# Attention and two feed-forward layers on one core: PSUM as eight one-bank tiles behind the first product, another sharing of the first pair's banks, and later squares

## The chip, the cores and the metric

The kernel runs on one core of one Trainium2 chip. Its engines are TensorE (PE in the profile), VectorE (DVE), ScalarE (ACT), GpSimd (POOL) and SyncE (SP, which here only starts loads and stores). They run side by side and meet at semaphores. The metric is the time of one execution on the device in microseconds. The kernel before takes 766.9 us (median of 3 runs, 766.66 to 767.11).

## The reference

```python
def _attn_ref(q, k, v, centroids):          # q, k, v: 2 x 8 x 768 x 64
    ...                                     # q_n, k_n, c_n: normalised rows
    q_assign = np.argmax(np.einsum('bhsd,hcd->bhsc', q_n, c_n), axis=-1)
    k_assign = np.argmax(np.einsum('bhsd,hcd->bhsc', k_n, c_n), axis=-1)
    mask = q_assign[:, :, :, None] == k_assign[:, :, None, :]
    scores = np.where(mask, scale * np.matmul(q, k.transpose(0, 1, 3, 2)), -1e9)
    ...                                     # softmax over the last axis
    return np.matmul(attn, v)

def _moe_ref(x, w_in, w_out):               # x: 1536 x 512, w_in: 512 x 2048
    h = np.maximum(x @ w_in, 0.0)
    return h * h @ w_out

def _moe2_ref(x, w_in, w_out):
    h = x @ w_in
    g = h * (1.0 / (1.0 + np.exp(-1.702 * h)))
    return g @ w_out
```

The attention's output, 1536 tokens of 512 numbers, goes through the first layer (relu, squared) and then through the second (a gelu). Each layer has a first product with `w_in` and a second one with `w_out`.

## The kernel before

**The order.** The kernel is written under a manual schedule. Each piece of work is recorded by `at(key, f, ...)`, all pieces are sorted by their key, and in that order they are issued to the engines. `moment(u)` turns a count of steps into a key; one step `u` of the two layers is 2.7 us of PE work. Each engine works its own instructions off in the order of their issue. What an instruction has to wait for is worked out while it is recorded, from the tiles that it reads and writes.

**The first layer's first product** (`first_hidden`, L831, with `first_product`, L787). `w_in` has 16 blocks of 128 columns, taken as eight pairs `j`. Each pair is computed by seven products of half-size blocks instead of eight, in the order P1, P2, P6, P5, P7, P3, P4. Every number is a sum of a high and a low part, so one product of 384 columns is six matmuls (`PASSES`). The results of the seven products run together in three accumulators: u (P1, P6, P7, P4 one after the other), c (P2) and x (P5, P3). Between them ACT copies an accumulator out (`first_take`, L811), or DVE adds it to a copy (`first_plus`, L816), and only then PE goes on adding into it. ACT also does the relus (L819, L823, and L827 with Relu) and the squares (L827 with Square). In pair 0 the two batches b are done one after the other, with 384 columns each; from pair 1 on both come together, twelve matmuls a product, and one copy or add takes both (768 elements).

**PSUM.** A partition of PSUM has eight banks of 512 numbers. The attention uses tiles of two banks (`ps_s`) and of one. For batch 0 of pair 0 the first product borrows two `ps_s` tiles (named `ps_h`), with u and c in the two banks of one and x in the other. Then `open_banks` (L760) closes the attention's pool and opens four tiles of two banks, `row0` to `row3`; `banks[i]` is half of `row{i // 2}`. For batch 1 of pair 0, u and c are the two halves of `row0` and x is a half of `row1`; from pair 1 on u, c and x are a whole row tile each. Everything behind, that is both second products (`reduce_out`, L976 to L981) and the second layer's first product (`product`, L869, for two of three column blocks, and `plain`, L878, for the third), uses single halves as accumulators, with ACT and DVE reading out (L886, L889, L883; L990, L1010, L1014, L1025).

**The weights** come as 64-bit numbers and are turned into a high and a low part on the way (`pair_stages`, L250 to L305): ACT L270, DVE L273 to L284, then ACT L288 and a difference L291 on POOL or DVE (the raw halves), four sums L296, ACT L299 and a difference L302. Pairs 0 and 1 have L291, L296 and L302 on POOL, the others on DVE. `PAIR_N` (L67) holds the keys of these steps; `rest_2` are those of L288, L291, L296, L299 and L302 of pair 2.

The second products split their moving operand in the same way: ACT L964 writes the high part, DVE L968 the low part, and PE reads both.

Of the kernel before, what the change touches and what calls it, by code (L numbers as in the profile page):

```python
# [8 lines left out]
F32 = mybir.dt.float32  # L9
# [3 lines left out]
AF = mybir.ActivationFunctionType  # L13
# [54 lines left out]
    load=-4.0, steps_1=(-1.0, -0.3, -0.2, -0.1, 0.0), steps_2=(-0.55, -0.3, 0.0, 0.3, 0.6), steps=(-1.95, -1.25, -0.9, -0.35, 0.0),  # L68
    rest_1=(3.2, 3.5, 3.7, 4.28, 4.5), rest_2=(1.0, 1.3, 1.95, 3.1, 4.1), rest=(0.85, 1.2, 1.95, 2.6, 3.0),
)  # L70
# [12 lines left out]
def cluster_attention_then_two_ffns(  # L83
# [224 lines left out]
    with tc.manual_schedule():  # L308
        with ExitStack() as actx:
            psum = actx.enter_context(tc.tile_pool(name="psum", bufs=1, space=bass.MemoryType.PSUM))  # L310
# [449 lines left out]
            def open_banks():  # L760
                actx.close()
                pool = ctx.enter_context(tc.tile_pool(name="psum2", bufs=1, space=bass.MemoryType.PSUM, reuse_waits="tile"))
                rows.extend(pool.tile([P, 2, CH], F32, name=f"row{i}") for i in range(4))
                banks.extend(rows[i // 2][:, i % 2, :] for i in range(8))

# [8 lines left out]
            def first_sum(name, j, b):  # L774
                i = "ucx".index(name)
                if j:
                    return first_banks(j)[i][:, b, :HALF]
                if b:
                    return banks[i][:, :HALF]
                if (i // 2, "early") not in ps_u:  # L780
                    ps_u[i // 2, "early"] = ps_s("ps_h")
                return ps_u[i // 2, "early"][:, i % 2, :HALF]

# [47 lines left out]
            def first_hidden(u0):  # L831
                cursor = u0
                for j in range(MJ):
                    for group in (((0,), (1,)) if j == 0 else ((0, 1),)):
                        b = group[0] if len(group) == 1 else None
                        for name in FIRST_ORDER:
                            for x in group:
                                at(moment(cursor), first_product, name, j, x)
                                cursor += BLOCK
                            end = cursor  # L840
                            if name in ("P1", "P6", "P5"):
                                at(moment(end + 0.02), first_take, name, j, b)
                            elif name in ("P2", "P7", "P3"):
                                at(moment(end + 0.02), first_plus, name, j, b)
                                if name == "P7":
                                    at(moment(end + 0.36), first_relu, 1, j, 1, b)
                                if name == "P3":
                                    at(moment(end + 0.36), first_whole, 0, j, b, AF.Relu)
                                    at(moment(end + 0.9), first_whole, 0, j, b, AF.Square)
                            else:  # L850
                                at(moment(end + 0.02), first_relu_banked, name, j, b)
                                at(moment(end + 1.2), first_whole, 1, j, b, AF.Square)

# [189 lines left out]
            at(moment(7 * BLOCK) - 0.01, open_banks)  # L1043
            first_hidden(u0)
            for j in range(MJ):
                places_ = ((32 * KB, 40 * KB), (26 * KB, 34 * KB))[j] if j < 2 else (98 * KB, 106 * KB) if j % 2 else (0, 8 * KB)
# [127 lines left out]
```

## Time and profile before

| | |
|---|---|
| median of 3 runs | 766.9 us |
| profiled execution | 766.83 us |
| its span, first to last instruction | 765.0 us |
| mean granted clock of TensorE | 0.999 |
| PE busy | 750.6 us (98%) |
| DVE, ACT, POOL busy | 525.5, 461.8, 165.6 us |
| L981, both second products | 262.4 us of PE |
| L793, first layer's first product | 110.9 us of PE in `row` tiles, 8.5 in `ps_h` |
| L869 and L878, second layer's first product | 81.8 and 48.2 us of PE |

PE is busy nearly all the time, so the table says which stretches are long, and not what a change in one of them is worth. A matmul here lasts longer than the distance to the next (389 ns of 128x512 against some 227), because matmuls overlap in the array. A stretch is therefore judged by its length over its number of matmuls, and a stall by how much longer it is than a free stretch. The attention ends and the first product begins near 250 us, the first layer's second product begins at 376.5, the second layer's first product at 507.8, its second one at 628.9.

### The profile page before, as it was taken

How to read it: one execution, taken by the hardware profiler on the slowest of the kernel's cores; microseconds unless marked ns; L12 is line 12 of the kernel's file. 1: busy time of each engine (PE TensorE's matmuls, PEld its weight loads, DVE VectorE, ACT ScalarE, POOL GpSimd, SP SyncE). 2: the span in 40 equal slices, each digit the busy share in tenths (PEclk: the TensorE clock that was granted, in tenths of full speed). 3: DMA queues.
4: the chain of work that ended last, by engine and by line, in shares of the span. 5: the costliest groups of instructions: out<-in, count | busy, mean ns of one | idle time of the engine just before them, and what ended most of it. 6: DMA issues, size and time to landing. Idle time of an engine off the chain costs nothing.

```text
span 765.0 us, 10778 instructions
## 1 busy us (share of the span) xinstructions
PE 750.6 (98%) x3995; PEld 605.3 (79%) x3995; DVE 525.5 (69%) x939; ACT 461.8 (60%) x800; POOL 165.6 (22%) x139
## 2 busy tenths in 40 slices
PE   8899999999999999999999999999999999999997
PEld 5677776766767789999988887888888878888786
DVE  6876866867886567665777768744777667776321
ACT  7877777786777567776854435545656554443321
POOL 3764756774758130000000000000000000000000
PEclk9999999999999999999999999999999999999999
DMA  5132321322320221301222320100212213230201
GB/s 187 43 104 56 96 79 42 101 72 56 96 87 3 73 93 56 111 4 53 82 99 96 111 83 15 41 23 34 82 56 84 82 56 98 95 111 28 110 1 55
DMA packets 17044, 54.53 MB, mean 71 GB/s; under 512 B 2592, under 2 KB 2848, under 8 KB 15968
## 3 DMA queue, kind: packets, MB, share of 16 engines
q1 hardware_dynamic: 16704, 53.32, 21.6%
q8 instruction: 31, 0.51, 0.3%
q10 hardware_dynamic: 288, 0.52, 0.2%
q14 instruction: 21, 0.17, 0.1%
HBM read 43.02 MB, written 3.15 MB: 60 GB/s over the span
## 4 chain that ended last, share of the span: by engine, by line
PE 86%; DVE 7%; ACT 4%; issue 1%; POOL 1%; DMA 0%; DVEq 0%; ACTq 0%; POOLq 0%
PE row L981 32%; PE row L793 11%; PE row L869 10%; PE ps_v L649 8%; PE ps_p L631 7%; PE row L878 5%; PE ps_s L606 5%; PE ps_s L609 4%; DVE arena L615 1%; PE ps_aff L467 1%; ACT arena L623 1%; PE ps_r L666 1%; PE ps_back L484 1%; ACT arena L827 1%; DVE arena L997 1%
## 5 line engine op out<-in xcount | busy, mean ns | idle before, releaser
L981 PE MATMUL row<-arena 128*128 128x512 f32 x1152 | 262.4, 389 | 0.7 <-DVE arena L1025 0.6
L981 PEld LDWEIGHTS row<-arena 128*128 128x128 f32 x1152 | 215.9, 188 | 46.8 <-DVE arena L1025 1.0
L615 DVE TENSOR_SCALAR_CACHE_REDUCE arena<-ps_s 128x768 bf16<-128x768 f32 x96 | 91.7, 955 | 39.1 <-PE ps_s L609 11.4
L793 PE MATMUL row<-arena 128*128 128x384 f32 x630 | 110.9, 335 | 2.1 <-ACT arena L811 2.1
L793 PEld LDWEIGHTS row<-arena 128*128 128x128 f32 x630 | 109.0, 188 | 3.8 <-ACT arena L811 3.7
L964 ACT CAST arena<-arena 128x512 fp32r<-128x512 f32 x96 | 59.4, 620 | 86.2 <-PE row L981 85.9
L623 ACT ACTIVATE arena<-ps_s,arena 128x768 f32<-128x768 f32 x96 | 87.2, 908 | 36.1 <-DVE arena L615 35.8
L968 DVE TENSOR_TENSOR arena<-arena,arena 128x512 fp32r<-128x512 f32 x96 | 66.1, 689 | 60.2 <-ACT arena L964 60.0
L869 PE MATMUL row<-arena 128*128 128x512 f32 x336 | 81.8, 391 | 0.2 <-DVE arena L889 0.2
L869 PEld LDWEIGHTS row<-arena 128*128 128x128 f32 x336 | 62.7, 188 | 14.8 <-DVE arena L889 1.3
L649 PE MATMUL ps_v<-arena 128*64 128x384 f32 x384 | 72.3, 498 | 0.0
L631 PE MATMUL ps_p<-arena 128*128 128x128 f32 x576 | 70.8, 272 | 0.0
L244 ACT CAST arena<-arena 128x512 fp32r<-128x512 f32 x48 | 29.8, 620 | 64.4 <-DVE arena L240 64.4
L631 PEld LDWEIGHTS ps_p<-arena 128*128 128x128 f32 x576 | 65.7, 141 | 2.3 <-issue 0.6
L606 PE MATMUL ps_s<-arena 128*128 128x384 f32 x192 | 54.8, 366 | 2.5 <-ACT arena L623 2.4
L609 PE MATMUL ps_s<-arena 80*128 80x384 f32 x192 | 49.9, 340 | 0.1
L247 DVE TENSOR_TENSOR arena<-arena,arena 128x512 fp32r<-128x512 f32 x48 | 33.2, 692 | 24.2 <-ACT arena L244 23.4
L878 PE MATMUL row<-arena 128*128 128x512 f32 x192 | 48.2, 390 | 0.0
L606 PEld LDWEIGHTS ps_s<-arena 128*128 128x128 f32 x192 | 31.1, 189 | 20.5 <-ACT arena L623 10.1
L639 DVE COPY arena<-ps_p 128x512 f32<-128x512 f32 x72 | 47.0, 678 | 0.2 <-PE ps_p L631 0.2
L649 PEld LDWEIGHTS ps_v<-arena 128*64 128x64 f32 x384 | 23.4, 136 | 25.5 <-issue 25.2
L827 ACT ACTIVATE arena<-arena 128x1536 f32<-128x1536 f32 (+1 forms) x27 | 36.3, 1346 | 10.1 <-DVE arena L816 10.1
(133 smaller groups left out, 953.0 us busy)
## 6 DMA issues: line engine op xcount, KB each, us to landing
arena<-in_w_dram SPq DMA_DIRECT2D x48, 512.0 KB, 3.2
arena<-in_w_dram SPq DMA_DIRECT2D x8, 1024.0 KB, 4.8
arena<-arena SPq DMA_DIRECT2D x32, 192.0 KB, 2.6
arena<-in_k_t_dram SPq DMA_DIRECT2D x8, 384.0 KB, 3.8
arena<-in_v_dram SPq DMA_DIRECT2D x8, 384.0 KB, 3.3
out_dram<-arena SPq DMA_DIRECT2D x11, 256.0 KB, 2.1
arena<-in_q_t_dram SPq DMA_DIRECT2D x7, 384.0 KB, 3.4
arena<-arena SPq DMA_DIRECT2D x28, 48.0 KB, 2.1
```

The costliest lines, as they stand in the source:

```text
L606: nc.tensor.matmul(ps[:, n, :HALF], lhsT=x_s[i][:, t * P:(t + 1) * P], rhs=k1_s[i][:, n * HALF:(n + 1) * HALF], start=True, stop=False)
L609: nc.tensor.matmul(ps[:, n, :HALF], lhsT=q2_s[i][:, t * P:(t + 1) * P], rhs=k2_s[i][:, n * HALF:(n + 1) * HALF], start=False, stop=True)
L615: nc.vector.tensor_scalar(out=unused, in0=s_t[g][:, :, :HALF], scalar1=-scale, scalar2=None, op0=ALU.mult, op1=ALU.min, accum_out=m_t[g])
L623: nc.scalar.activation(out=p_t[g].rearrange("p (n f) -> p n f", n=2), in_=s_t.pop(g)[:, :, :HALF], func=AF.Exp, bias=m_t.pop(g), scale=sca ...
L631: nc.tensor.transpose(ps[:, x * P:(x + 1) * P], p_t[2 * k + j][:, t * P:(t + 1) * P], ident)
L649: nc.tensor.matmul(pv_t[n][j * D:(j + 1) * D, :HALF], lhsT=raw[n // 2, "v"][:, j, t, :], rhs=pt_t[n, j][:, t, :], start=(t == 0), stop=(t ...
L793: nc.tensor.matmul(ps, lhsT=w[:, a, (off + x) * P:(off + x + 1) * P], rhs=FIRST_MOVING[moving, b][x][:, e, :], start=(n == 0 and name in ( ...
L869: nc.tensor.matmul(ps, lhsT=w[:, a, off + x * P:off + (x + 1) * P], rhs=MOVING[moving][x][:, b, :], start=(n == 0 and name in ("P1", "P2", ...
L878: nc.tensor.matmul(ps, lhsT=w[:, a, kk * P:(kk + 1) * P], rhs=THIRD_CHUNK[kk][:, b, :], start=(n == 0), stop=(n == 11), skip_group_check=True)
L964: nc.scalar.copy(out=half_of(layer, n)[:, 0, :], in_=g_t[m][:, c, :])
L968: nc.vector.tensor_tensor(out=t[:, 1, :], in0=g_t[m][:, c, :], in1=t[:, 0, :].bitcast(F32), op=ALU.subtract)
L981: nc.tensor.matmul(ps, lhsT=lhsT, rhs=rhs, start=(m == 0 and e == 0), stop=(m == MF - 1 and e == 2))
```

## The change

Three things change. First, the accumulators of pair 0 are shared out otherwise: u has a two-bank tile to itself, c and x are the two halves of another. Second, when the first layer's first product is over, the four row tiles are given back and eight tiles of one bank each take their place at the same addresses (`split_banks`). Third, in pairs 0, 1 and 2 the second layer of work on a copied block, relu and square, gets later keys (`later`: 3, 2 and 1 steps), and pair 2's weight split gets later keys too (`rest_2`). The relu that reads an accumulator itself (`first_relu_banked`) is recorded a little earlier, so that in the last pair it comes before the pool is closed. The added lines shift the names of lines by up to 7: L793, L811, L816, L819, L823 and L827 of before are L798, L816, L821, L824, L828 and L832 of the changed kernel, and L981 is L987.

```diff
-    rest_1=(3.2, 3.5, 3.7, 4.28, 4.5), rest_2=(1.0, 1.3, 1.95, 3.1, 4.1), rest=(0.85, 1.2, 1.95, 2.6, 3.0),
+    rest_1=(3.2, 3.5, 3.7, 4.28, 4.5), rest_2=(2.33, 2.4, 2.5, 3.2, 4.1), rest=(0.85, 1.2, 1.95, 2.6, 3.0),
...
             def open_banks():
                 actx.close()
-                pool = ctx.enter_context(tc.tile_pool(name="psum2", bufs=1, space=bass.MemoryType.PSUM, reuse_waits="tile"))
+                pool = rctx.enter_context(tc.tile_pool(name="psum2", bufs=1, space=bass.MemoryType.PSUM, reuse_waits="tile"))
                 rows.extend(pool.tile([P, 2, CH], F32, name=f"row{i}") for i in range(4))
-                banks.extend(rows[i // 2][:, i % 2, :] for i in range(8))
+
+            def split_banks():
+                rctx.close()
+                pool = ctx.enter_context(tc.tile_pool(name="psum3", bufs=1, space=bass.MemoryType.PSUM, reuse_waits="tile"))
+                banks.extend(pool.tile([P, CH], F32, name=f"bank{i}") for i in range(8))
...
                 if b:
-                    return banks[i][:, :HALF]
-                if (i // 2, "early") not in ps_u:
-                    ps_u[i // 2, "early"] = ps_s("ps_h")
-                return ps_u[i // 2, "early"][:, i % 2, :HALF]
+                    return rows[(i + 1) // 2][:, i // 2, :HALF]
+                t = (i + 1) // 2, "early"
+                if t not in ps_u:
+                    ps_u[t] = ps_s("ps_h")
+                return ps_u[t][:, i // 2, :HALF]
...
+                later = (3.0, 2.0, 1.0) + (0.0,) * MJ
...
-                                    at(moment(end + 0.36), first_relu, 1, j, 1, b)
+                                    at(moment(end + 0.36 + later[j]), first_relu, 1, j, 1, b)
...
-                                    at(moment(end + 0.36), first_whole, 0, j, b, AF.Relu)
-                                    at(moment(end + 0.9), first_whole, 0, j, b, AF.Square)
+                                    at(moment(end + 0.36 + later[j]), first_whole, 0, j, b, AF.Relu)
+                                    at(moment(end + 0.9 + later[j]), first_whole, 0, j, b, AF.Square)
...
-                                at(moment(end + 0.02), first_relu_banked, name, j, b)
-                                at(moment(end + 1.2), first_whole, 1, j, b, AF.Square)
+                                at(moment(end - 0.02 * (j == MJ - 1) + 0.01), first_relu_banked, name, j, b)
+                                at(moment(end + 1.2 + later[j]), first_whole, 1, j, b, AF.Square)
...
+            at(moment(y0 - 0.005), split_banks)
```

PE, POOL and SP issue their instructions in the same order as before; DVE swaps one pair of neighbours (pair 1's L816 on c now stands before pair 2's L291).

ACT at batch 0 of pair 0, before, with what each waits for (`ps_h` 2570 holds u and c, 2614 x; L811 are the copies of u behind P1 and P6 and of x behind P5):

```order
L811 COPY arena_112640_59<-ps_h_2570 128x384 [waits PE_49]
L670 COPY arena_112640_59<-ps_r_2579 128x384
L811 COPY arena_112640_59<-ps_h_2570 128x384 [waits DVE_49]
L695 CAST arena_114688_58<-arena_112640_59 128x384 [waits DVE_49]
L811 COPY arena_112640_59<-ps_h_2614 128x384 [waits PE_49]
```

And in the changed kernel (2570 holds u, 2592 c and x):

```order
L816 COPY arena_112640_59<-ps_h_2570 128x384 [waits PE_49]
L670 COPY arena_112640_59<-ps_r_2579 128x384 [waits PE_49]
L816 COPY arena_112640_59<-ps_h_2570 128x384 [waits PE_49]
L695 CAST arena_114688_58<-arena_112640_59 128x384 [waits DVE_49]
L816 COPY arena_112640_59<-ps_h_2592 128x384 [waits PE_49]
```

The order is the same; the second copy of u waits for PE and no longer for DVE's add.

ACT from pair 1's raw weights (L288) to pair 1's first copy of u (`row_2665`, 768 elements), before (`row_2663` and `row_2664` are rows 0 and 1, with batch 1 of pair 0):

```order
L288 CAST arena_58<-arena_59 128x768
L827 ACTIVATE arena_59<-arena_59 128x768
L811 COPY arena_59<-row_2663 128x384
L827 ACTIVATE arena_59<-arena_59 128x768
L811 COPY arena_59<-row_2664 128x384
L299 CAST arena_58<-arena_59 128x1024
L270 ACTIVATE arena_59<-arena_59 128x1024
L823 ACTIVATE arena_59<-arena_59 128x384
L827 ACTIVATE arena_59<-arena_59 128x768
L819 ACTIVATE arena_59<-row_2663 128x384
L827 ACTIVATE arena_59<-arena_59 128x768
L811 COPY arena_59<-row_2665 128x2x384
```

And in the changed kernel (rows 0, 1 and 2 are 2661, 2662 and 2663):

```order
L288 CAST arena_58<-arena_59 128x768
L816 COPY arena_59<-row_2661 128x384
L816 COPY arena_59<-row_2662 128x384
L299 CAST arena_58<-arena_59 128x1024
L270 ACTIVATE arena_59<-arena_59 128x1024
L828 ACTIVATE arena_59<-arena_59 128x384
L824 ACTIVATE arena_59<-row_2661 128x384
L832 ACTIVATE arena_59<-arena_59 128x768
L816 COPY arena_59<-row_2663 128x2x384
```

Before, four relus and squares of 768 elements (L827) stand between L288 and the copy, now one (L832), and it is batch 0's.

PE where the second layer's last column block begins (L981, from the last matmuls of the block before it), before; `row_2663` to `row_2666` are rows 0 to 3:

```order
L981 MATMUL row_2666<-arena_58 128x512 x3
L981 MATMUL row_2663<-arena_58 128x512 [waits Activation_49]
L981 MATMUL row_2663<-arena_58 128x512 x2
L981 MATMUL row_2666<-arena_58 128x512 [waits DVE_49]
L981 MATMUL row_2666<-arena_58 128x512 x2
L981 MATMUL row_2665<-arena_58 128x512 x6
L981 MATMUL row_2663<-arena_58 128x512 [waits Activation_49]
```

And in the changed kernel (`bank_3507` to `bank_3514` are banks 0 to 7):

```order
L987 MATMUL bank_3514<-arena_58 128x512 x3
L987 MATMUL bank_3508<-arena_58 128x512 x3
L987 MATMUL bank_3513<-arena_58 128x512 x3
L987 MATMUL bank_3511<-arena_58 128x512 [waits Activation_49]
L987 MATMUL bank_3511<-arena_58 128x512 [waits DVE_49]
L987 MATMUL bank_3511<-arena_58 128x512
L987 MATMUL bank_3512<-arena_58 128x512 [waits DVE_49]
```

The last six matmuls of the old block (banks 1 and 6) wait for nobody; the new block's first ones wait for the readers of their own banks.

## Rows read from the trace of the kernel before

**Rows 1.** The page: busy time; costliest groups (busy, mean ns | idle before, releaser)
```profile
PE 750.6 (98%) x3995; PEld 605.3 (79%) x3995; DVE 525.5 (69%) x939; ACT 461.8 (60%) x800; POOL 165.6 (22%) x139
...
L981 PE MATMUL row<-arena 128*128 128x512 f32 x1152 | 262.4, 389 | 0.7 <-DVE arena L1025 0.6
...
L793 PE MATMUL row<-arena 128*128 128x384 f32 x630 | 110.9, 335 | 2.1 <-ACT arena L811 2.1
```
**Rows 2.** The waits of PE: us in total, times, longest
```profile
PE row L793 <- ACT arena L811: 2.1, 5, 0.8
```
**Rows 3.** Timeline of PE, first products: start, length, instructions, count [idle before, releaser]
```profile
254.52 1.32 PE L793 MATMUL ps_h<-arena 128*128 128x384 f32 x6
...
257.85 2.38 PE L793 MATMUL ps_h<-arena 128*128 128x384 f32 x12
260.40 3.43 PE L793 MATMUL ps_h<-arena 128*128 128x384 f32 x18 [0.17 <-ACT arena L811]
263.68 2.24 PE L793 MATMUL row<-arena 128*128 128x384 f32 x12
266.49 2.36 PE L793 MATMUL row<-arena 128*128 128x384 f32 x12 [0.57 <-ACT arena L811]
269.04 7.65 PE L793 MATMUL row<-arena 128*128 128x384 f32 x42 [0.19 <-ACT arena L811]
277.47 4.46 PE L793 MATMUL row<-arena 128*128 128x384 f32 x24 [0.79 <-ACT arena L811]
282.09 10.68 PE L793 MATMUL row<-arena 128*128 128x384 f32 x60 [0.16 <-ACT arena L811]
...
293.17 83.50 PE L793 MATMUL row<-arena 128*128 128x384 f32 x480 [0.41 <-ACT arena L811]
```
**Rows 4.** Timeline of ACT, first products
```profile
255.87 0.48 ACT L811 COPY arena<-ps_h 128x384 f32<-128x384 f32 x1 [0.60 <-PE ps_h L793]
...
259.87 0.48 ACT L811 COPY arena<-ps_h 128x384 f32<-128x384 f32 x1 [3.14 <-DVE arena L816]
...
265.96 0.48 ACT L811 COPY arena<-row 128x384 f32<-128x384 f32 x1
266.33 0.84 ACT L288 CAST arena<-arena 128x768 fp32r<-128x768 f32 x1
...
274.80 0.83 ACT L827 ACTIVATE arena<-arena 128x768 f32<-128x768 f32 x1
...
276.64 0.79 ACT L811 COPY arena<-row 128x768 f32<-128x768 f32 x1
...
290.96 1.48 ACT L827 ACTIVATE arena<-arena 128x1536 f32<-128x1536 f32 x1
```
**Rows 5.** Timeline of DVE, first pair
```profile
259.28 0.56 DVE L816 TENSOR_TENSOR arena<-ps_h,arena 128x384 f32<-128x384 f32 x1 [4.25 <-issue]
```
**Rows 6.** Timeline of PE, the first layer's second product
```profile
376.51 131.42 PE L981 MATMUL row<-arena 128*128 128x512 f32 x576
```
**Rows 7.** Timeline of DVE where the first layer's last column block begins
```profile
464.41 0.69 DVE L990 COPY arena<-row 128x512 f32<-128x512 f32 x1 [0.67 <-ACT arena L990]
...
477.43 0.69 DVE L968 TENSOR_TENSOR arena<-arena,arena 128x512 fp32r<-128x512 f32 x1
```
**Rows 8.** The chain that ended last: start, length, what; second layer's first product
```profile
513.39 3.03 PE row L869 x12
...
519.14 2.72 PE row L869 x12
...
543.77 3.01 PE row L869 x12
...
619.02 1.54 PE row L878 x6
...
627.41 1.65 PE row L869 x6
```
**Rows 9.** Timeline of PE, the second layer's last column block
```profile
716.09 44.50 PE L981 MATMUL row<-arena 128*128 128x512 f32 x195 [0.63 <-DVE arena L1025]
```

More of the change, by code (lines that the diff above doesn't have):

```diff
@@ L308, in cluster_attention_then_two_ffns @@
     with tc.manual_schedule():
-        with ExitStack() as actx:
+        with ExitStack() as actx, ExitStack() as rctx:
             psum = actx.enter_context(tc.tile_pool(name="psum", bufs=1, space=bass.MemoryType.PSUM))
```

## The prediction

> **What bounds the kernel now.** Read the page first: its busy table, then its costliest groups. TensorE (PE) is busy 750.6 us of a span of 765.0 us [rows 1], so a change is worth only what it takes out of PE's idle time or puts into it. The two groups that matter here show 2.1 us of idle time before L793 (the first layer's first product) and 0.7 us before L981 (the second products of both layers) [rows 1]; the table of waits names who ends it: ScalarE (ACT), five times [rows 2]. That understates the loss, since idle time counts only from the modelled end of a matmul. So go on to PE's timeline and compare stretches with their own free pace. A free stretch of 384 columns is the last row of [rows 3]: 480 matmuls in 83.50 us, less one duration of 0.335 [rows 1] and 0.11 for a slow second matmul, over 479 steps, is 0.1734 us a step. From 257.85, 660 matmuls (12, 18, 12, 12, 42, 24, 60, 480) should take 114.7 us with the last one's overlap and one restart; they end at 376.67, after 118.8. **Some 4.1 us are lost in the first products, all before 293.2** [rows 3].
>
> Why, is read from ACT and VectorE (DVE). In the first pair u and c lie in one two-bank tile. ACT's copy of u (P1's result) at 255.87 waited for PE [rows 4], and what PE had just ended was P2, into the other bank (254.52 + 1.32 = 255.84, [rows 3]). ACT's next copy waited 3.14 us for a DVE add [rows 4], which reads the other bank from 259.28 on for 0.56 us [rows 5], and which had itself started only after P6 into u's bank. So who waits for whom goes by tile, not by bank, and reader behind reader too.
>
> The same shows behind the first products. DVE's copy of one bank at 464.41 had stood 0.67 us behind ACT's copy of the neighbour; DVE then has a queue until the split at 477.43 for which PE waits [rows 7]. The first part of L981 takes 131.42 us for 576 matmuls [rows 6]; at 0.2267 a step (2.72 us for 12, [rows 8]) and 0.39 for the last [rows 1] it would be 130.74: 0.68 us lost. In the second layer's first product PE's regular 2.72 and 1.36 become 3.03, 3.01 (after 0.15 idle), 1.54 and 1.65 [rows 8]: 0.31 + 0.44 + 0.18 + 0.29 = 1.22 us. And at 716.09, where the second layer's last part begins, PE was idle for 0.63 us [rows 9]; with the 0.16 by which matmuls normally overlap and 0.11 for the restart that is 0.90.
>
> **The change part by part.** No arithmetic is added or removed. PE, POOL and SP (with all loads) keep their order, DVE swaps two neighbours, ACT moves the relus and squares of the first three pairs back. What changes most is the waits.
>
> *First pair's banks.* u is alone in a tile; c and x share one. ACT's copy behind P6 waits for P6 alone and ends at 259.2 + 0.48 = 259.7; P7 follows P5 without a gap, at 257.85 + 0.11 + 12 x 0.1734 = 260.04 instead of 260.40 [rows 3]. The new wait is that P5 (x) stands behind DVE's add on c; that add can start at P2's end, 255.9, and P5 comes at 259.0. Queued behind the add on DVE are the last attention tile's product and the T splits, and these move forward with it. In the second half of the pair ACT takes u when P1 ends, 264.4, not at 265.96 [rows 4]; P6 comes at 265.3 and finds it done. The stalls at 260.40, 266.49 and 269.04 go; the waits that follow have 0.2 to 0.3 us to spare.
>
> *Pair 1's first copy* is late next. Its chain is a weight split: ACT L288 (266.33), a difference and four sums on POOL, ACT L299, then in ACT's queue four instructions besides L270 before the copy at 276.64 [rows 4]. From L288's start to the copy's start that is 10.31 us. In the changed order three stand there, one L827 less: 0.83 us long, less 0.1 by which neighbours on ACT overlap (265.96 + 0.48 against 266.33, [rows 4]), 0.73. L288 itself follows P1's copy, which starts at 264.4, so it starts at 264.8. So pair 1's copy starts at 264.8 + 10.31 - 0.73 = 274.4 and ends 0.79 later, at 275.2; PE, which arrives at 260.04 + 84 x 0.1734 = 274.6, waits 0.6 and pays 0.11. Before, it restarted at 277.47 [rows 3]. Bounds of this wait: none, if L288 starts 0.6 earlier than I think; 2.1 us, if it stays at 266.33.
>
> *Behind it.* Pair 1's P6 copy now stands ahead of L288 (the new `rest_2`), not behind L288's wait for DVE: P6 ends at 277.6, the copy at 278.4, and P7 wants it at 279.5. L288 then runs at 278.4, and the add that DVE now does ahead of L291 costs nothing, since what L291 gives is wanted by pair 2's P1 at 275.3 + 60 x 0.1734 = 285.7. In pair 2, P1's copy ends at 288.8; a relu and L288 of 0.75 each and two squares of 1.4 (L827 at 290.96, [rows 4]) bring ACT to 293.0, P6's copy ends at 293.8, and P7 wants it at 294.1. These 0.3 us are the smallest margin; beyond it the moved squares cost their length. The other moved squares lie in ACT's idle time, and their results are read by the second products much later.
>
> From pair 1's P6 on no stall is left: 275.2 + 0.11 + 564 x 0.1734 + 0.16 = 373.3 against 376.67. **First products: 3.4 us.**
>
> *One bank a tile afterwards.* DVE's copy of [rows 7] waits for its own product alone, so its queue moves 0.6 us forward, and PE's wait at its end is some 0.45 (the rest of the 0.68 is restarts). I take the whole **0.68**; 0 is the other end. In the second layer's first product P6 no longer waits for the add on c12 at 513.39 and 543.77, the third column's product at 619 not for the gelu's reading of its neighbour bank, and the add before P4 at 627 not for P2. The true dependences end about 0.5 us or more before PE comes: **1.22**, with 0 as the other end. At 716.09 PE waited for DVE's copy of the neighbour; now it waits there for nothing: **0.90**. The first L981 gets two waits instead of one, both long satisfied; the nearest row is the idle time of 0.15 before the matmul at 543.77, which also has two [rows 8]. That costs between 0 and 0.15 and cannot give time back; I take 0.1. The end is not touched: the last two half copies still share one bank and stay in turn.
>
> The Trainium skill's page PSUM — Partial Sum Buffer, section "PSUM bank collisions raise a hardware error", says that two engines must not touch one bank and quadrant at once, two reads included, while accesses to different banks run clean. The row [rows 4] shows ACT held by DVE across two banks, which is more than the rule asks; by the rule one bank a tile removes that wait (760.8), by the row taken as the chip's own behaviour it stays (763.5, the second rival).
>
> Sum: 3.4 + 0.68 + 1.22 + 0.90 - 0.1 = 6.1 us. The profiled execution took 766.83 us, 1.83 outside its span; the median of the runs is 766.9, 0.07 more. 766.9 - 6.1 = 760.8.
>
> **The rivals.**
> 1. *The weight split clamps pair 1.* L288 does not start before 266.3, say because the T splits ahead of it wait for DVE. For it: L288 to copy is a chain of hand-overs with no slack [rows 4]. Against: by the sum above all that stands ahead of L288 ends earlier. Pair 1 then gains only 0.73 us: 1.5 us of the sum are gone, 762.3.
> 2. *Splitting tiles frees nothing behind the first products,* because ACT and DVE cannot read neighbouring banks side by side or the queues are late by themselves: 766.9 - 3.4 = 763.5. Against: at 464.41 and 716.09 the engine named as the releaser worked on another bank [rows 7, 9].
> 3. *The moved squares come in the way: slower.* ACT runs in order; one square of 1.4 us [rows 4] ahead of each of the three copies of pairs 1, 2 and 3 lands on PE once the margin is used up. Nine times 1.4, less a margin of 0.4 each, is 9 us; less 2.7 gained behind, 766.9 + 6.3 = 773.2. With half as many it is still 768.7. It decides once ACT comes some 0.3 us late to the copy at 293. For it: that margin, and a queue in which L288 waits for DVE. Against: pair 3 has its old order again, in which 480 matmuls ran without a gap [rows 3].
> 4. *Nothing changes,* since what is freed at one restart is only waited for at the next: 766.9. Against: the free stretch behind 293.17 [rows 3], in which an earlier start is kept.
>
> **How the numbers follow.** Forecast 0.73 (its own range is 760.1, if pair 1's stall goes too, to 761.5, if the 0.68 does not come), rival 1 0.11, rival 2 0.08, rivals 3 and 4 0.04 each. The range of 760.0 to 762.9 takes in the forecast's bounds and rival 1, and goes half of the way from there to rival 2. 0.2%, what a measurement can tell from no change, is 1.5 us: the forecast and rivals 1 and 2 are faster (0.92), rival 4 the same (0.04), rival 3 slower (0.04).
>
> **What would show it.** In the profile after: DVE's add behind P2 starts before 256; P7 at 260.0; one stall left from there to pair 2, at 275.2, ended by ACT's copy; L981 starts at 373.3, and its first 576 matmuls take 130.7; no idle time of 0.6 where the last part begins, near 710; the second layer's first product without rows of 3.0. The prediction is wrong if PE loses over 1 us between 258 and 300, if it waits for ACT in pair 2 or 3, or if L981's first part still takes 131.4.

## The result, and the profile after

The changed kernel takes 759.68 us (median of 4 runs, 759.54 to 759.91), the kernel before, run beside it, 766.78 us (766.47 to 767.11). The ratio is 0.9908, with a 95% interval of 0.9890 to 0.9925. The sign and the places were forecast; the time lies 1.1 us below the forecast of 760.8 and 0.3 us below the low end of its range. The profiled execution after took 759.55 us, its span 757.7 us; before 766.83 and 765.0. So 7.28 us are to be found between the two traces.

First the page after: the busy table, and of the costliest groups the two that [rows 1] shows of before (L981 is now L987, L793 now L798). Further down, L869 of before is L875, and L990, L1022, L1023, L1025 and L1026 have become L996, L1028, L1029, L1031 and L1032.

```profile
PE 746.8 (99%) x3995; PEld 606.4 (80%) x3995; DVE 525.8 (69%) x939; ACT 461.6 (61%) x800; POOL 165.5 (22%) x139
...
L987 PE MATMUL bank<-arena 128*128 128x512 f32 x1152 | 261.5, 389 | 0.0
...
L798 PE MATMUL row<-arena 128*128 128x384 f32 x630 | 109.7, 334 | 0.4 <-ACT arena L816 0.4
```

Both second products have lost all their idle time, the first products all but 0.4 us. The timeline of PE through the first products (start, length, instructions, count, idle time before and its releaser) answers to [rows 3]:

```profile
257.60 5.50 PE L798 MATMUL ps_h<-arena 128*128 128x384 f32 x30
262.94 11.64 PE L798 MATMUL row<-arena 128*128 128x384 f32 x66
...
274.96 98.08 PE L798 MATMUL row<-arena 128*128 128x384 f32 x564 [0.38 <-ACT arena L816]
```

Six breaks have become one, the one forecast for pair 1, and 564 matmuls follow without another. On ACT the same stretch shows who makes it:

```profile
264.18 0.48 ACT L816 COPY arena<-row 128x384 f32<-128x384 f32 x1 [0.55 <-PE row L798]
264.56 0.84 ACT L288 CAST arena<-arena 128x768 fp32r<-128x768 f32 x1
...
272.60 0.51 ACT L828 ACTIVATE arena<-arena 128x384 f32<-128x384 f32 x1
273.02 0.47 ACT L824 ACTIVATE arena<-row 128x384 f32<-128x384 f32 x1
273.39 0.83 ACT L832 ACTIVATE arena<-arena 128x768 f32<-128x768 f32 x1
274.12 0.79 ACT L816 COPY arena<-row 128x768 f32<-128x768 f32 x1
```

ACT takes u when P1 ends and begins L288 at 264.56; pair 1's copy starts at 274.12, with three instructions ahead of it. From there on PE has three rows that matter, which answer to [rows 6, 8, 9]: the first layer's second product, the start of the second layer's first product, and the second layer's second product.

```profile
372.89 130.80 PE L987 MATMUL bank<-arena 128*128 128x512 f32 x576
503.52 8.32 PE L875 MATMUL bank<-arena 128*128 128x512 f32 x36
...
623.20 130.72 PE L987 MATMUL bank<-arena 128*128 128x512 f32 x576
```

Between the second and the third row the timeline shows no idle time. The last row runs through the place at which PE was idle for 0.63 us before [rows 9]. Two rows of DVE answer to [rows 5, 7]. The add behind P2 now starts at P2's end. And the copy that stood behind ACT's copy of the neighbour waits for PE alone and comes 0.6 us earlier, counted from the product's start (460.17 - 372.89 = 87.28, before 464.41 - 376.51 = 87.90):

```profile
255.68 0.56 DVE L821 TENSOR_TENSOR arena<-ps_h,arena 128x384 f32<-128x384 f32 x1 [0.89 <-ACT arena L816]
...
460.17 0.69 DVE L996 COPY arena<-bank 128x512 f32<-128x512 f32 x1 [0.67 <-PE bank L987]
```

DVE's queue behind it moves with it: the split at 477.43 of [rows 7] begins at 473.18 after, 0.63 us earlier by the same count. What the forecast did not have is the end. The timeline of before from 759 us on, ACT, DVE and the queues SPq and ACTq that issue the stores:

```profile
759.27 1.27 ACT L1025 COPY arena<-row 128x512 f32<-128x512 f32 x2 [6.18 <-PE row L981]
759.88 1.54 SPq L1026 DMA_DIRECT2D out_dram<-arena  x3
759.89 0.69 DVE L1025 COPY arena<-row 128x512 f32<-128x512 f32 x1 [6.07 <-ACT arena L1025]
760.63 0.37 ACT L1022 COPY arena<-row 128x256 f32<-128x256 f32 x1
...
761.03 0.42 DVE L1022 COPY arena<-row 128x256 f32<-128x256 f32 x1 [0.45 <-ACT arena L1022]
761.52 0.45 SPq L1023 DMA_DIRECT2D out_dram<-arena  x1
```

And after:

```profile
751.92 0.59 ACT L1031 COPY arena<-bank 128x512 f32<-128x512 f32 x1 [5.50 <-PE bank L987]
752.54 1.69 SPq L1032 DMA_DIRECT2D out_dram<-arena  x3
752.60 0.69 DVE L1031 COPY arena<-bank 128x512 f32<-128x512 f32 x1 [5.45 <-PE bank L987]
...
753.96 0.37 ACT L1028 COPY arena<-bank 128x256 f32<-128x256 f32 x1
...
754.37 0.42 DVE L1028 COPY arena<-bank 128x256 f32<-128x256 f32 x1 [1.07 <-ACT arena L1028]
754.82 0.33 SPq L1029 DMA_DIRECT2D out_dram<-arena  x1
```

The last bank's two half copies stay in turn, as forecast: ACT's at 760.63, DVE's 0.40 later; after 753.96 and 0.41 later. But from the start of ACT's one to the end of the span it takes 765.0 - 760.63 = 4.37 us before and 757.7 - 753.96 = 3.74 after. What moved are the copies of the part's first two banks, which shared a tile. ACT's copy of the first starts 1.36 us ahead of its last one before (759.27) and 2.04 after (751.92); DVE's copy of the second, which stood behind ACT's, 0.74 us before (759.89) and 1.36 after (752.60), where it waits for PE alone. The first store follows ACT's copy. The last store then lands sooner, as the list of DMA issues shows (KB each, us from issue to landing), first before, then after:

```profile
out_dram<-arena SPq DMA_DIRECT2D x1, 128.0 KB, 2.6
```

```profile
out_dram<-arena SPq DMA_DIRECT2D x1, 128.0 KB, 2.0
```

### The profile page after: what moved, and what is told of

It is laid out like the page before. It is cut to its first block, busy times and chain, and to the rows that moved or that the text cites. A ratio compares the mean times of both kernels' runs of the same rounds, so it can differ in the third digit from the quotient of the medians.

```text
span 757.7 us, 10782 instructions
## 1 busy us (share of the span) xinstructions
PE 746.8 (99%) x3995; PEld 606.4 (80%) x3995; DVE 525.8 (69%) x939; ACT 461.6 (61%) x800; POOL 165.5 (22%) x139
## 2 busy tenths in 40 slices
DMA packets 17044, 54.53 MB, mean 72 GB/s; under 512 B 2592, under 2 KB 2848, under 8 KB 15968
## 4 chain that ended last, share of the span: by engine, by line
PE 91%; DVE 4%; ACT 3%; POOL 1%; issue 1%; DMA 0%; DVEq 0%; POOLq 0%; ACTq 0%
PE bank L987 34%; PE row L798 13%; PE bank L875 10%; PE ps_v L649 8%; PE ps_p L631 7%; PE bank L884 6%; PE ps_s L606 4%; PE ps_s L609 4%; DVE arena L615 2%; PE ps_h L798 1%; PE ps_aff L467 1%; ACT arena L623 1%; PE ps_r L666 1%; PE ps_back L484 1%; PE ps_oh L550 1%
## 5 line engine op out<-in xcount | busy, mean ns | idle before, releaser
L987 PE MATMUL bank<-arena 128*128 128x512 f32 x1152 | 261.5, 389 | 0.0
L987 PEld LDWEIGHTS bank<-arena 128*128 128x128 f32 x1152 | 216.2, 188 | 44.9 <-DVE arena L974 0.2
L798 PE MATMUL row<-arena 128*128 128x384 f32 x630 | 109.7, 334 | 0.4 <-ACT arena L816 0.4
L798 PEld LDWEIGHTS row<-arena 128*128 128x128 f32 x630 | 109.2, 188 | 0.7 <-ACT arena L816 0.7
L875 PE MATMUL bank<-arena 128*128 128x512 f32 x336 | 80.9, 389 | 0.0
L875 PEld LDWEIGHTS bank<-arena 128*128 128x128 f32 x336 | 63.1, 188 | 13.1
L884 PE MATMUL bank<-arena 128*128 128x512 f32 x192 | 48.1, 389 | 0.0
L639 ACT COPY arena<-ps_p 128x512 f32<-128x512 f32 x72 | 41.9, 582 | 0.6 <-PE ps_p L631 0.5
```

The source lines that it names most:

```text
L639: (nc.scalar.copy if on_act else nc.vector.tensor_copy)(out=pt_t[n][:, 4 * b:4 * b + 4, i * P:(i + 1) * P], in_=tp_t.pop((k, b)).rearrange ...
L798: nc.tensor.matmul(ps, lhsT=w[:, a, (off + x) * P:(off + x + 1) * P], rhs=FIRST_MOVING[moving, b][x][:, e, :], start=(n == 0 and name in ( ...
L875: nc.tensor.matmul(ps, lhsT=w[:, a, off + x * P:off + (x + 1) * P], rhs=MOVING[moving][x][:, b, :], start=(n == 0 and name in ("P1", "P2", ...
L884: nc.tensor.matmul(ps, lhsT=w[:, a, kk * P:(kk + 1) * P], rhs=THIRD_CHUNK[kk][:, b, :], start=(n == 0), stop=(n == 11), skip_group_check=True)
L987: nc.tensor.matmul(ps, lhsT=lhsT, rhs=rhs, start=(m == 0 and e == 0), stop=(m == MF - 1 and e == 2))
```

## The experiments

My theory after the comparison: the change is three separate things. The edits to the first products give 3.4 us there; one-bank tiles give 0.6 + 1.5 + 1.0 us behind; and they give 0.6 us at the end, because in a two-bank tile the copy of the last part's first bank waits for the product into its neighbour, so the stores start late and the last one lands behind them. The rivals: the parts hide each other; the shorter end is a store that landed sooner by chance. Each time below stands beside runs of the kernel before on the same chip. Their medians lie between 766.48 and 766.64 us where the changed kernel's stood beside 766.78, so a difference against the changed kernel is good to some 0.3 us; where it is smaller, stretches of the traces are compared. "First products" below means the stretch from the start of PE's last piece in `ps_h` behind the attention (257.85 before) to the first second product (376.51): 118.66 us before, 115.29 after.

**Each part of the change alone**

**e1.** The first pair's banks only:

```diff
-                    return banks[i][:, :HALF]
-                if (i // 2, "early") not in ps_u:
-                    ps_u[i // 2, "early"] = ps_s("ps_h")
-                return ps_u[i // 2, "early"][:, i % 2, :HALF]
+                    return rows[(i + 1) // 2][:, i // 2, :HALF]
+                t = (i + 1) // 2, "early"
+                if t not in ps_u:
+                    ps_u[t] = ps_s("ps_h")
+                return ps_u[t][:, i // 2, :HALF]
```

> The kernel before with the new sharing of the first pair's banks alone (u alone in a tile, c with x); relus and squares, and everything behind the first products, as before. My theory: the stalls of TensorE at 260.40, 266.49 and 269.04 go (0.45 + 0.84 + 0.46 us), L288 moves some 1.5 us forward, and with it pair 1's copy, so of the wait before 277.47 only some 0.3 us is gained or lost; at pair 1's restart the kernel is 1.5 us ahead. The stalls at 282.09 and 293.17 (0.43 and 0.68) stay, since their cause is ScalarE's order. 766.8 - 1.5 = 765.3 us. Rival (what is gained early is only waited for at pair 1's copy and behind): 766.8. Rival (the sharing alone does it all): 763.4.

Measured: 766.09 us, before 766.61, ratio 0.9993 (0.9984 to 1.0002): 0.5 us less, which the interval does not tell from none. In the trace the first products take 375.60 - 257.46 = 118.14 us, 0.52 less. My 1.5 us did not come. PE's timeline tells why (behind the edit e1's lines are numbered one above those of before):

```profile
257.46 5.53 PE L794 MATMUL ps_h<-arena 128*128 128x384 f32 x30
262.82 2.25 PE L794 MATMUL row<-arena 128*128 128x384 f32 x12
265.56 9.69 PE L794 MATMUL row<-arena 128*128 128x384 f32 x54 [0.48 <-ACT arena L812]
276.54 4.46 PE L794 MATMUL row<-arena 128*128 128x384 f32 x24 [1.30 <-ACT arena L812]
```

The breaks at 260.40 and 269.04 are gone, but the one of 266.49 is back at 265.56 and pair 1's wait has grown from 0.79 [rows 3] to 1.30. On ACT a relu of 768 elements (L828) and the relu of P4 (L820) stand ahead of the copy of u:

```profile
263.91 0.85 ACT L828 ACTIVATE arena<-arena 128x768 f32<-128x768 f32 x1 [0.89 <-DVE arena L817]
264.66 0.47 ACT L820 ACTIVATE arena<-ps_h 128x384 f32<-128x384 f32 x1
265.03 0.47 ACT L812 COPY arena<-row 128x384 f32<-128x384 f32 x1
265.39 0.85 ACT L288 CAST arena<-arena 128x768 fp32r<-128x768 f32 x1
...
275.70 0.79 ACT L812 COPY arena<-row 128x768 f32<-128x768 f32 x1
```

So L288 starts at 265.39 and pair 1's copy only at 275.70, where I had put them at 264.8 and 275.1. PE ends its work ahead of that copy 1.05 us earlier (265.56 + 9.69 - 257.46 = 17.79, before 269.04 + 7.65 - 257.85 = 18.84) and restarts only 0.54 earlier (19.08, before 19.62): half of what it has gained by then is given back while the relus and squares stand where they stood.

**e3.** The later squares and `rest_2` only:

```diff
-    ... rest_2=(1.0, 1.3, 1.95, 3.1, 4.1), ...
+    ... rest_2=(2.33, 2.4, 2.5, 3.2, 4.1), ...
...
+                later = (3.0, 2.0, 1.0) + (0.0,) * MJ
...
-                                    at(moment(end + 0.9), first_whole, 0, j, b, AF.Square)
+                                    at(moment(end + 0.9 + later[j]), first_whole, 0, j, b, AF.Square)
```

(and the same for the two relus and the other square)

> The kernel before with the later relus and squares of pairs 0 to 2 and the new order of pair 2's weight split alone; all banks shared as before. My theory: the stalls at 260.40, 266.49 and 269.04 stay; pair 1's copy comes 0.7 us sooner (one square less ahead of it), and the stalls at 282.09 and 293.17 (0.43 and 0.68) go: 1.8 us, 765.0. Rival (without the earlier start of L288 the moved squares only come in the way of the copies behind): 766.8 or above. Rival (this part does it all): 763.4.

Measured: 764.72 us, ratio 0.9975 (0.9965 to 0.9985): 1.9 us, as expected, and in the trace the first products take 374.49 - 257.70 = 116.79 us, 1.87 less. The breaks at 260.25, 266.33 and 268.87 stay; those of pair 1's P7 and of pair 2 are gone. Pair 1's first copy starts at 275.71 instead of 276.64, and its wait no longer shows as a break of its own.

**e4.** Both, with two-bank tiles behind:

> The kernel before with both edits to the first products (sharing and squares) and two-bank tiles behind them as before. My theory: the first products gain the 3.4 us that they gain in the changed kernel, and nothing behind them changes: 763.4 us; the end stays 4.8 us long. Rival (the later stages give some of it back, being paced by weight loads): between 763.4 and 766.8. If e1 and e3 are 1.5 and 1.8 below the kernel before and this one 3.4, the two parts simply add up.

Measured: 763.27 us, ratio 0.9955 (0.9943 to 0.9968): 3.3 us, as expected, and more than the 0.5 and 1.9 of the parts. In the traces it is 3.37 (372.85 - 257.56 = 115.29) against 0.52 and 1.87. So the parts do not simply add up, as I had assumed when I gave each its own share of the 3.4: the sharing is worth 0.5 alone and 1.5 once the squares are out of the way (3.37 - 1.87).

**e2.** One-bank tiles only (`split_banks` as in the change, the first pair's old sharing and the old keys):

> The kernel before with one-bank tiles from the first layer's second product on, and nothing else of the change. My theory: 0.63 in that product's first part, 1.45 in the second layer's first product, 0.98 up to and with the start of the last part, and 0.61 at the end, together 3.7: 763.1 us. Rival 1 (the shorter end of the changed kernel is a store that happened to land sooner): 763.7, with 4.8 us from the last matmul's start to the end of the span. Rival 2 (splitting frees nothing): 766.8. The first products are those of before, 118.8 us from 257.85 on.

Measured: 762.96 us, ratio 0.9952 (0.9939 to 0.9964): 3.65 us. Its last store lands after 2.0 us, like that of the changed kernel, though its first products take 118.66 us as before (376.33 - 257.67). With e4's 3.3 that is 7.0, the whole 7.1.

**The end**

**e5.** Two-bank tiles again, from the second layer's second product on:

```diff
...
+            def join_banks():
+                bctx.close()
+                pool = ctx.enter_context(tc.tile_pool(name="psum4", ...))
+                joined = [pool.tile([P, 2, CH], F32, name=f"joined{i}") for i in range(4)]
+                banks[:] = [joined[i // 2][:, i % 2, :] for i in range(8)]
...
+            at(moment(y1 - 0.005), join_banks)
```

(`split_banks` opens its pool so that it can be closed again, and the gelu that reads the last accumulator ahead of the new tiles is recorded 0.06 of a step earlier, so that it reads the old tile)

> The changed kernel, but from the second layer's second product on the banks are again four tiles of two. My theory: TensorE waits again at the start of the last part (0.93 us) and the end is again longer by 0.6, since the copy of the last part's first bank waits for the product into its neighbour: 759.7 + 1.5 = 761.2 us. Rival (the shorter end was a store that landed sooner by chance, or the earlier finish of TensorE): the end stays 4.2 us, 760.6. Rival (the wait at the last part's start is only moved): 759.7 to 760.3.

Measured: 761.28 us, 1.6 above the changed kernel, ratio 0.9929 (0.9916 to 0.9941). In the trace 0.95 us is lost up to ACT's last half copy (755.15 - 623.44 = 131.71, after 753.96 - 623.20 = 130.76) and 0.71 from there to the end (759.6 - 755.15 = 4.45, after 3.74). PE's wait is back at the start of the last part, and the last store lands after 2.6 us again:

```profile
710.62 44.50 PE L993 MATMUL joined<-arena 128*128 128x512 f32 x195 [0.63 <-DVE arena L1037]
```

```profile
out_dram<-arena SPq DMA_DIRECT2D x1, 128.0 KB, 2.6
```

**e6.** The end alone, without touching PE or the tiles:

```diff
+                if c == 2 and i == 0:
+                    nc.scalar.copy(out=o[:, :1], in_=sums(1, c, 1)[:, :1])
+                if c == 2 and i == 1:
+                    nc.vector.tensor_copy(out=o[:, :1], in_=sums(1, c, 0)[:, :1])
```

> The changed kernel with one-bank tiles throughout; only in the last part ScalarE reads one column of the second bank before it copies the first, and VectorE one column of the first before it copies the second. So both copies wait as they did with two-bank tiles, and TensorE is not touched. My theory: the stores start 0.6 to 0.8 us later and the end is as much longer: 760.4 us. Rival (the landing of the last store does not depend on when the earlier ones left): no difference, 759.7, and 4.2 us from the last matmul's start to the end.

Measured: 760.56 us, 0.9 above the changed kernel, ratio 0.9920 (0.9906 to 0.9933). ACT's last half copy, DVE's and the queue of SP show where it goes:

```profile
753.14 1.79 SPq L1036 DMA_DIRECT2D out_dram<-arena  x3
...
753.69 0.37 ACT L1028 COPY arena<-bank 128x256 f32<-128x256 f32 x1
...
754.10 0.42 DVE L1028 COPY arena<-bank 128x256 f32<-128x256 f32 x1
755.02 0.49 SPq L1029 DMA_DIRECT2D out_dram<-arena  x1
```

```profile
out_dram<-arena SPq DMA_DIRECT2D x1, 128.0 KB, 2.6
```

The held copies make the stores late; the last one goes 0.09 us behind the three others (753.14 + 1.79 = 754.93), where the changed kernel has 0.59, and lands after 2.6 instead of 2.0. PE is as after up to ACT's last half copy (753.69 - 622.94 = 130.75). From there to the end it takes 758.5 - 753.69 = 4.81 us, 1.07 more than after and 0.4 more than two-bank tiles cost. The edit overshoots: its two extra readings delay the second bank's copy further (it starts 0.29 us ahead of ACT's last one, at 753.40, where it was 0.74 before), and the last store, ready at 754.52 when DVE ends, is issued only at 755.02, behind the three. So e6 shows that late copies alone lengthen the end, and not by how much two-bank tiles do.

That size is read from the runs together. From the start of ACT's last half copy to the end of the span, the kernels with two-bank tiles there (before, e1, e3, e4, e5) take 4.37 to 4.45 us, and those with one-bank tiles and nothing else altered in the last part (after, e2, e7, e9) 3.74 to 3.80. So the shorter end is neither chance nor an earlier finish of TensorE: it comes with the freed copies.

**Is what remains to be had?**

**e7.** The first pair's relus and squares put off further (`later = (4.5, 2.0, 1.0)`):

> The changed kernel with the first pair's relus and squares put off further (4.5 in place of 3.0): ahead of pair 1's first copy stand only L270 and the relu out of PSUM. My theory: the copy starts 1.1 us sooner, TensorE's wait of 0.54 at 274.96 and the 0.11 behind it go: 759.0 us. Rival (the squares then delay the next copies, so that the wait comes back in pair 1 or 2): 759.7 or above.

Measured: 759.46 us, ratio 0.9905 (0.9892 to 0.9919), 0.2 below the changed kernel instead of 0.65. The rival was right: the wait at 274.96 is gone, and another has come at pair 1's P7, 0.39 us long by the free pace (281.20 - 263.12 - 102 x 0.1734).

```profile
263.12 17.86 PE L798 MATMUL row<-arena 128*128 128x384 f32 x102
281.20 19.05 PE L798 MATMUL row<-arena 128*128 128x384 f32 x108 [0.23 <-ACT arena L816]
```

The first products take 372.89 - 257.78 = 115.11 us, 0.18 less than after. Two squares now stand between L288 and the copy for which PE waits, while ACT had been idle for 1.77 us ahead of the copy before that:

```profile
276.85 0.80 ACT L816 COPY arena<-row 128x768 f32<-128x768 f32 x1 [1.77 <-PE row L798]
278.15 0.83 ACT L288 CAST arena<-arena 128x768 fp32r<-128x768 f32 x1 [0.50 <-DVE arena L284]
278.89 1.58 ACT L832 ACTIVATE arena<-arena 128x768 f32<-128x768 f32 x2
280.38 0.77 ACT L816 COPY arena<-row 128x768 f32<-128x768 f32 x1
```

**e8.** The same with the last two steps of the last part taken bank by bank:

```diff
+                            last = layer == 1 and c == 2 and m >= MF - 2
...
-                                at(moment(u + 0.25 * i), reduce_out, layer, n, m, c, i)
+                                when = u + 0.25 * i if not last else u - (m - MF + 2) + 0.5 * i + 0.25 * (m - MF + 2)
+                                at(moment(when), reduce_out, layer, n, m, c, i)
...
-                            ends = u + 0.25 * (i - 3) - (part[-1] - c)
+                            ends = u + (0.5 if layer == 1 and c == 2 else 0.25) * (i - 3) - (part[-1] - c)
```

> As the kernel with the relus put off further, and in addition the last two steps of the last part are done bank by bank (six matmuls into one bank, then the next), so the four banks are finished 1.36 us apart and not 0.68. Same matmuls, same sums. My theory (the end is the time in which 1 MB of stores drains, so what leaves early shortens it): the end goes from 4.2 to some 3.7 us, 758.5. Rival 1 (the last store has a fixed landing time): no gain, 759.0. Rival 2 (the last step's halves, now wanted 2 us sooner, are late): TensorE waits up to 2 us, 759.5 to 761.

Measured: 759.29 us, ratio 0.9903 (0.9888 to 0.9918): 0.17 below e7, not 0.5. My theory that the end is the draining of 1 MB falls in its size: the first store leaves at 750.49, 2 us sooner, and the end hardly follows. What goes with the landing time is how close the store ahead of the last one is:

```profile
750.49 3.05 SPq L1032 DMA_DIRECT2D out_dram<-arena  x3
...
754.81 0.33 SPq L1029 DMA_DIRECT2D out_dram<-arena  x1
```

```profile
out_dram<-arena SPq DMA_DIRECT2D x1, 128.0 KB, 1.7
```

From the end of the three on SP to the start of the last there are 1.27 us here. All stores ahead left earlier too, so this run does not separate the distance from the amount still under way.

**e9.** Between the two settings of the squares (`later = (4.2, 2.0, 1.0)`), one square fills ACT's gap:

> The changed kernel with the first pair's relus and squares put off by 4.2 in place of 3.0. Against 4.5 one square of 0.75 us moves from between L288 and the copy at 280.38 into the idle 1.77 us of ScalarE ahead of the copy at 276.85. My theory: the copy for which TensorE waited 0.39 us at 281.20 comes 0.73 sooner, so that wait and the 0.10 behind it go, and none is left in the first products: 0.5 us below the kernel with 4.5, 0.65 below the changed one, 759.0. Rival (the copy is late because L288 waits for VectorE, not because of the squares): 759.5, as with 4.5.

Measured: 758.88 us, before 766.48, ratio 0.9900 (0.9886 to 0.9915). As expected, the first products have no break left and take 372.04 - 257.40 = 114.64 us, 0.65 less than after:

```profile
257.40 5.50 PE L798 MATMUL ps_h<-arena 128*128 128x384 f32 x30
262.74 109.47 PE L798 MATMUL row<-arena 128*128 128x384 f32 x630
```

**e10.** e9 with the edit of e8:

> As the kernel with 4.2, and the last two steps of the last part done bank by bank. My theory now (the last store lands 1.7 us after its issue where the store ahead of it left 2 us earlier, 2.0 where it left 0.9 earlier, 2.6 where it left 0.5 earlier): 0.2 us below the kernel with 4.2, 758.8. Rival (the 0.17 between the two earlier kernels was scatter): the same as with 4.2, 759.0.

Measured: 758.63 us (758.55 to 759.07), ratio 0.9899 (0.9882 to 0.9915). It is the lowest median, but its runs overlap with e9's (758.70 to 759.14). What speaks for a real gain is the landing of 1.7 us, the same as in e8 (in both the store ahead is issued 1.60 us before the last one, not 2 as I had put it), and the time from the last store's issue to the end of the span: 756.8 - 754.16 = 2.64 us, in e9 756.9 - 753.97 = 2.93. Against the changed kernel both intervals overlap; there the breaks in PE's timeline carry the claim, not the times.

## Why the prediction was right and where it was wrong

**First products: right.** Forecast 3.4, measured 3.37 (before 376.51 - 257.85 = 118.66, after 372.89 - 257.60 = 115.29, the stretch named above). DVE's add behind P2 started at 255.68, as forecast before 256, and P7 followed without a gap. The changed kernel starts this stretch 0.25 us earlier, for a reason outside the change (below), so its times read 0.25 lower: L288 was forecast at 264.8 and began at 264.56, pair 1's copy at 274.4 and began at 274.12, the one stall at 275.2 and it came at 274.96, 0.58 long by the free pace (274.96 - 262.94 - 66 x 0.1734) where 0.6 was forecast. One slip: the 373.3 at which L981 was to start is where the last matmul ends; by the same sum (275.2 + 0.11 + 564 x 0.1734) the product starts at 373.1, and it did at 372.89. This sum did not test the parts: e1 showed that the sharing without the squares is worth 0.5 us, a third of what it is worth with them. Rivals 1, 3 and 4 did not occur in the changed kernel, but they lie close by. In e1 L288 is late, as in rival 1, and half of what is gained early is waited for at pair 1's copy, as in rival 4; in e7 squares stand ahead of a copy and PE waits, as in rival 3.

**One bank a tile, behind the first products: right, two sizes off.** First part of L987: forecast 0.68, measured 0.63 (before 507.77 - 376.51 = 131.26 to the start of L869, after 503.52 - 372.89 = 130.63). Second layer's first product: forecast 1.22, measured 1.45 (before 628.90 - 507.77 = 121.13, after 623.20 - 503.52 = 119.68): beside the four slow rows of [rows 8] the chain has smaller ones (2.81 at 573.98 and 2.80 at 603.99 in place of 2.72, and some of 0.02), which I had not counted. Second layer's second product: forecast 0.90 for the start of its last part, measured 0.97 up to ACT's last half copy (760.63 - 628.90 = 131.73, after 753.96 - 623.20 = 130.76). The two waits at the first L987 were to cost 0.1 and cost nothing. The starts of before:

```profile
507.77 4.47 PE L869 MATMUL row<-arena 128*128 128x512 f32 x19
...
628.90 86.57 PE L981 MATMUL row<-arena 128*128 128x512 f32 x381
```

Rival 2, that splitting frees nothing, is out by e2: 3.65 us from it alone. What the Trainium skill's page PSUM — Partial Sum Buffer, section "PSUM bank collisions raise a hardware error", allows, engines side by side on different banks, the trace after agrees with: ACT copies the first bank from 751.92 to 752.51 while PE goes on into the neighbour without a break.

**The step that failed: "The end is not touched".** I put the end at nothing and gave it no bounds, since I looked at the last bank alone, whose two half copies do stay in turn. But the part's first two banks shared a tile as well: ACT's copy of the first bank waited for the product into the second, and DVE's copy of the second for ACT's, the very rule I applied at every other place. After, ACT's copy comes 0.68 us sooner against its last one and DVE's 0.62, the stores with them, the last store lands after 2.0 instead of 2.6 us, and the end is 0.63 us shorter. e5 brought this back together with PE's wait, 0.71 of its 1.6 us being the end; e6 held the copies alone, more than two-bank tiles do, and lost 0.9. Without the 0.63 the time would have been 760.3, inside my range. Why a last store close behind another takes longer to land stays open.

**The sum.** 3.37 + 0.63 + 1.45 + 0.97, 0.63 at the end and 0.25 ahead of the change are 7.30, the 7.28 between the profiled runs but for rounding. The forecast was 6.1. Of the difference the end is 0.6, the uncounted small rows 0.2, the two waits 0.1, and 0.25 is no effect of the change. With the same attention ahead, PE's last piece in `ps_h` starts anywhere between 257.34 (e6) and 257.85 (before); e5 and e7, which do the same up to there as the changed kernel, have 257.84 and 257.78 where after has 257.60. My range ended at 760.0, since but for pair 1's stall it held only terms that could fail, and none that I might have missed on the other side.

## What to carry to other kernels

When a wait goes by tile, list every place at which two users share a tile, and go through all of them, the last copies before the stores too: what ends a kernel has no later stage to hide in. Parts that feed one in-order queue are to be costed together: here 0.5 and 1.9 us alone are 3.3 us together, because part of what the first frees is given back behind the relus and squares that the second moves. And work put off must have a place to land: one square more between L288 and a copy cost 0.39 us of PE's time in e7, and nothing in e9, where it lay in the idle gap of 1.77 us before them.

## What the runs showed of the hardware

The same last store of 128 KB, issued from SP, landed after 2.6 us where 0.09 to 0.10 us lay between the end of the three stores ahead of it on SP and its own start (before, e1, e3, e4, e5, e6), 2.0 with 0.59 (after, e2, e7, e9), and 1.7 with 1.27 (e8, e10). The Trainium skill's page DMA: Bandwidth & Descriptors, section "Anatomy of one DMA — SWDGE (gpsimd) path", gives some 2.0 us of fixed cost and bytes over 436 GB/s for transfers issued by GpSimd; for 128 KB that would be 2.3, an estimate by that page. No row here is of that path; on SP's queue 1.7 was possible. Whether the distance itself counts, or how much is still under way when the last store is issued, was not separated.
